# First value loads between weight pieces, rounding one piece ahead, a later input audit and a later flag product, in a fused recurrence and MLP kernel

## The chip, the cores and the metric

The kernel runs on one core of a Trainium2 chip. Its time is the device time of one execution in microseconds (us), given as the median of several runs. The profile of one execution gives the "span", from the first to the last instruction, which is about 2 us shorter than the device time. Engines: PE is TensorE, DVE is VectorE, ACT is ScalarE, POOL is GpSimd, SP issues the transfers.

## The reference

```python
# q, k, v, alpha: (4, 8, 768, 48), float32
for t in range(S):
    state = alpha[:, :, t, :, None] * state + einsum('bhd,bhe->bhde', k[:, :, t], v[:, :, t])
    y[:, :, t] = einsum('bhd,bhde->bhe', q[:, :, t], state)
x = y.transpose(0, 2, 1, 3).reshape(3072, 384)
h = x @ w_in                     # (384, 2048)
out = (h * sigmoid(h)) @ w_out   # (2048, 384)
```

The two weights arrive as 8-byte floats and are rounded to 4 bytes on the chip.

## The kernel before

Attention works on 24 chunks of 128 tokens, in "steps" of four slots. Between the slots the MLP is woven in as pieces: `enter` pieces (x times w_in, then Silu) and `leave` pieces (times w_out). Four places matter.

The start: the first inputs, four pieces of w_in and, further down, two pieces of v are loaded on one queue.

```python
    load(0)
    load(1)
    for _ in range(4):
        fetch()                  # w_in pieces, 512 KB each
    # ... constants ...
    for n in range(NV):
        load_v(n)                # 192 KB each, in rows of 48 floats
```

The rounding of one weight piece takes one ACT and three DVE instructions:

```python
            tc.keep_in_program_order(act.activation(up, lo, AF.Copy, scale=2.0**-29))
            w = dst.bitcast(I32)
            tc.keep_in_program_order(
                dve.tensor_scalar(w, hi, 3, 0x3FFFFFFF, ALU.logical_shift_left, ALU.bitwise_and))
            dve.scalar_tensor_tensor(w, hi, -(1 << 30), w, ALU.bitwise_and, ALU.bitwise_or)
            dve.tensor_tensor(w, w, up, ALU.add)
            fetch()
            yield
```

The audit reads alpha and the weights once more (37 items) to see that all values lie in the range in which the fast algorithm is exact. It has one buffer, so each turn is a load, then one or two DVE reductions. Two turns a step run from the 13th step on; the rest runs in the tail, with one or two MLP pieces between two turns:

```python
        if at % 2 == 0 and step > 3 * GB:          # GB = 4
            next(audits, None)
    # ...
    turns = 0
    while next(audits, 0) is None:
        turns += 1
        for _ in range(1 + turns % 2):
            go_on()                                # one MLP piece
```

The flag: the audit's outcome is summed over the partitions by a tiny matmul; each engine then reads it to choose whether a general version must run as well.

```python
    dve.tensor_reduce(good, ends, axis=AX, op=ALU.min)
    go_on()
    go_on()
    ps = ps_attn()[0:1, 0, 0:1]
    pe.matmul(ps, lhsT=good, rhs=mask[:, 0, C - 1 : C], start=True, stop=True)
    dve.tensor_single_scalar(small, ps, 127.5, ALU.is_ge)
    for _ in range(4):
        go_on()
    within = nc.values_load(small[0:1, 0:1], min_val=0, max_val=1)
```

The compiler reorders each engine's instructions, so program order is only roughly kept, except where the program pins an instruction behind those before it.

## Time and profile before

| | before |
|---|---|
| device time, median of 3 | 569.04 us (568.75 to 571.14) |
| span of the profiled execution | 567.3 us |
| PE busy | 549.0 us (97%) |
| DVE busy | 445.0 us (78%) |
| ACT busy | 205.4 us (36%) |
| chain that ended last | PE 69%, DVE 17%, DMA 9% |

With PE busy for 97% of the span, only its gaps can be won, and time in which its clock is low. The prediction below shows the table of busy time by stretch, PE's waits and the clock around the flag. A line number such as L794 is a line of that kernel; the changed kernel's lines are shifted by about 7. A line of a view in order of time gives the start and the duration in us, the engine, the line, the operation, output<-input, how many instructions (x4), and in brackets how long the engine stood idle before it and for what. "Evacuation" is the copying of finished sums out of one of PE's output banks, after which PE can use the bank again; L889 is DVE's addition on the output of an `enter` piece.

### The profile page before, as it was taken

Reading aid. Unit: us, or ns where it says so; the run is one execution under the profiler, and the core shown is the slowest. Engines: PE = TensorE matmul, PEld = TensorE weight load, DVE = VectorE, ACT = ScalarE, POOL = GpSimd, SP = SyncE. Lnnn points to the kernel's source line nnn. Section 1 sums busy time; section 2 is a strip of 40 time slices with the busy share of each in tenths; the row PEclk is TensorE's granted clock in tenths of the full one; section 3 lists DMA queues with packets and bytes.
Section 4 is the critical chain, followed back from the end, with each engine's and each line's share of the span. In section 5 each row is a group of like instructions: output and inputs, shape, how many; then the busy total and the mean of one; then the engine's idle time right before and its main releaser. Section 6 shows DMA issues by size and latency. Waiting matters only on the chain.

```text
span 567.3 us, 12315 instructions
## 1 busy us (share of the span) xinstructions
PE 549.0 (97%) x5026; PEld 489.4 (86%) x5026; DVE 445.0 (78%) x815; ACT 205.4 (36%) x407; POOL 14.6 (3%) x36
## 2 busy tenths in 40 slices
PE   6899999999999999899999999999999999998996
PEld 4777887678999999799989999998999999997995
DVE  5797898488898599996998897999995866746531
ACT  3555543134323342443433443434443241421200
POOL 4111000100000000000000000000000000000000
PEclk9999999999999999999999999999999999998999
DMA  9989981533243324444425544425431223331000
GB/s 229 205 242 221 217 191 36 136 103 82 70 113 100 83 64 108 126 130 111 132 69 159 143 111 127 135 75 157 127 97 44 66 69 99 92 116 44 14 29 25
DMA packets 94415, 63.78 MB, mean 112 GB/s; under 512 B 55312, under 2 KB 86032, under 8 KB 94352
## 3 DMA queue, kind: packets, MB, share of 16 engines
q1 hardware_dynamic: 94352, 62.94, 43.1%
q8 instruction: 40, 0.66, 0.5%
q14 instruction: 23, 0.19, 0.1%
HBM read 58.20 MB, written 4.72 MB: 111 GB/s over the span
## 4 chain that ended last, share of the span: by engine, by line
PE 69%; DVE 17%; DMA 9%; SPq 2%; issue 1%; ACT 1%; DVEq 0%; ACTq 0%
PE ps_o L973 25%; PE ps_m L875 15%; PE ps_m L852 13%; DMA bits<-in_moe_w_out_dram 6%; PE ps_a L794 6%; PE ps_o L1000 4%; DVE seen L657 3%; PE ps_a L751 3%; DVE turn L668 1%; DMA vn<-in_v_dram 1%; PE ps_a L768 1%; DVE g L889 1%; DVE g L978 1%; DVE p L722 1%; PE ps_a L688 1%
## 5 line engine op out<-in xcount | busy, mean ns | idle before, releaser
L973 PE MATMUL ps_o<-w_out,g 128*128 128x192 f32 x704 | 122.4, 328 | 0.0
L973 PEld LDWEIGHTS ps_o<-w_out,g 128*128 128x128 f32 x704 | 115.3, 190 | 2.3 <-issue 0.4
L973 PE MATMUL ps_o<-wt,g 128*128 128x192 f32 x528 | 92.0, 328 | 0.0
L852 PE MATMUL ps_m<-xt,w_in 128*128 128x256 f32 x384 | 89.2, 383 | 1.3 <-DVE w_in L621 0.7
L973 PEld LDWEIGHTS ps_o<-wt,g 128*128 128x128 f32 x528 | 88.2, 192 | 1.4
L852 PEld LDWEIGHTS ps_m<-xt,w_in 128*128 128x128 f32 x384 | 70.9, 190 | 11.9 <-DVE w_in L621 1.6
L875 PE MATMUL ps_m<-xc,w_in 128*128 128x256 f32 x288 | 70.1, 379 | 1.4 <-DVE g L889 1.4
L875 PEld LDWEIGHTS ps_m<-xc,w_in 128*128 128x128 f32 x288 | 54.0, 190 | 7.9 <-DVE g L889 1.7
L886 ACT ACTIVATE g<-g 128x1024 f32<-128x1024 f32 x32 | 33.0, 1054 | 59.1 <-DVE g L889 59.1
L657 DVE TENSOR_REDUCE seen<-bits 128x1 f32<-128x384 int32 (+2 forms) x65 | 42.4, 687 | 15.1 <-DMA bits<-in_moe_w_out_dram 14.9
L875 PE MATMUL ps_m<-xc,wx 128*128 128x256 f32 x192 | 50.4, 384 | 0.0
L881 ACT COPY g<-ps_m 128x512 f32<-128x512 f32 x64 | 36.8, 586 | 36.2 <-PE ps_m L875 36.2
L978 DVE TENSOR_TENSOR g<-g 128x512 f32<-128x512 f32 x66 | 44.4, 683 | 7.0 <-PE ps_o L973 7.0
L774 ACT ACTIVATE st<-st,least 128x96 f32<-128x96 f32 x80 | 24.0, 365 | 59.1 <-DVE least L696 59.1
L889 DVE TENSOR_TENSOR g<-ps_m,g 128x512 f32<-128x512 f32 x56 | 37.1, 680 | 2.3 <-PE ps_m L875 2.1
L875 PEld LDWEIGHTS ps_m<-xc,wx 128*128 128x128 f32 x192 | 34.9, 190 | 4.2 <-issue 0.4
L693 DVE TENSOR_TENSOR_SCAN u<-al,one 128x516 f32<-128x516 f32 x24 | 29.0, 1209 | 9.0 <-ACT al L690 8.9
L855 ACT ACTIVATE g<-ps_m 128x512 f32<-128x512 f32 x32 | 19.1, 596 | 41.8 <-PE ps_m L852 41.6
L722 DVE TENSOR_TENSOR_SCAN p<-al,inv 128x516 f32<-128x516 f32 x24 | 29.4, 1227 | 5.0 <-PE ps_a L794 4.7
L762 DVE TENSOR_TENSOR g<-ps_a,mask 128x512 f32<-128x512 f32 x40 | 25.7, 684 | 9.0 <-PE ps_a L751 8.7
L794 PE MATMUL ps_a<-g,vn 128*32 128x128 f32 x768 | 27.2, 282 | 2.4 <-DMA vn<-in_v_dram 2.4
L794 PEld LDWEIGHTS ps_a<-g,vn 128*32 128x32 f32 x768 | 20.3, 112 | 10.1 <-issue 8.4
(127 smaller groups left out, 654.7 us busy)
## 6 DMA issues: line engine op xcount, KB each, us to landing
bits<-in_moe_w_in_dram SPq DMA_DIRECT2D x24, 512.0 KB, 4.7
bits<-in_moe_w_out_dram SPq DMA_DIRECT2D x32, 384.0 KB, 3.3
at<-in_alpha_dram SPq DMA_DIRECT2D x64, 96.0 KB, 2.3
kt<-in_k_dram SPq DMA_DIRECT2D x64, 96.0 KB, 2.4
qt<-in_q_dram SPq DMA_DIRECT2D x64, 96.0 KB, 2.5
bits<-in_alpha_dram SPq DMA_DIRECT2D x9, 512.0 KB, 3.6
out_dram<-o SPq DMA_DIRECT2D x48, 96.0 KB, 1.7
an<-in_alpha_dram SPq DMA_DIRECT2D x8, 192.0 KB, 5.1
```

The source lines that it names most:

```text
L657: dve.tensor_reduce(seen[kind][which][:, i : i + 1], x, axis=AX, op=op, apply_absolute_value=True))
L693: dve.tensor_tensor_scan(u[:, end - 1 :: -1], sg[:, end:0:-1], one[:, end:0:-1], 0.0, ALU.mult, ALU.add)
L722: dve.tensor_tensor_scan(p[:, 0:end], sg[:, 0:end], iv[:, 0:end], 0.0, ALU.mult, ALU.add)
L762: dve.tensor_tensor(g[:, u].rearrange("p (o j) c -> p o j c", o=2), ps[u].rearrange("p (o j) c -> p o j c", o=2), m.to_broadcast([128, 2, ...
L794: pe.matmul(py[32 * at : 32 * at + 32, t, :], lhsT=w, rhs=x, start=(i < 4), stop=(i >= len(todo) - 4), skip_group_check=True)
L852: pe.matmul(ps[:, e, :], lhsT=w_in[:, t, (f + e) * 128 : (f + e + 1) * 128], rhs=xt[:, t, :], start=(t == 0), stop=(t == NKT - 1))
L875: pe.matmul(ps[:, e], lhsT=block_w(w)[:, 2 * pair + e], rhs=block_x(grp, x), start=(first and e == 0), stop=(e == 1), skip_group_check=True)
L881: act.copy(to, ps)
L886: act.activation(x, x, AF.Silu)
L889: dve.tensor_tensor(to, a, b, op)
L973: pe.matmul(ps, lhsT=x, rhs=w[:, i], start=(first and i == 0), stop=(i == HF - 1), skip_group_check=True)
L978: dve.tensor_tensor(cells(grp, h, pair, *to), cells(grp, h, pair, *x), cells(grp, h, pair, *y), ALU.subtract)
```

## The change

The intent: the first v no longer stands behind four large transfers; DVE no longer waits for ACT's rounding of the same piece; the audit leaves the stretch in which DVE is the bound; and the flag's product comes when its input is long there.

```diff
     load(0)
     load(1)
-    for _ in range(4):
+    for i in range(4):
         fetch()
+        if i % 2 == 0:
+            load_v(i // 2)
...
-    for n in range(NV):
-        load_v(n)
...
-        for dst, src in pieces:
+        def rounding(bits):
+            n = bits.shape[1]
+            up = upp.tile([128, 512], I32, name="up")[:, 0:n]
+            tc.keep_in_program_order(
+                act.activation(up, bits.bitcast(U32)[:, :, 0], AF.Copy, scale=2.0**-29))
+            return up
+        ahead = []
+        for i, (dst, src) in enumerate(pieces):
...
             bits = coming.pop(0)
+            up = ahead.pop() if ahead else rounding(bits)
...   (the three DVE instructions, as before)
+            if i + 1 < len(pieces):
+                ahead.append(rounding(coming[0]))
             fetch()
             yield
...
-        if at % 2 == 0 and step > 3 * GB:
+        if at % 2 == 0 and step > 3 * GB + 2:
             next(audits, None)
...
-    go_on()
-    go_on()
+    for _ in range(5):
+        go_on()
     ps = ps_attn()[0:1, 0, 0:1]
     pe.matmul(ps, lhsT=good, rhs=mask[:, 0, C - 1 : C], start=True, stop=True)
```

## The prediction

> **What bounds the kernel now.** I read the page's busy shares first, then busy time by stretch, then what TensorE waited for, then the order of time around each wait. TensorE (PE) is busy 549.0 of 567.3 us (97%). The table by stretch shows where it is not; columns are stretch, length, then busy time (and instructions) of PE, its weight loads, VectorE (DVE), ScalarE (ACT), GpSimd, then granted clock, DMA share, GB/s.
>
> ```profile
> 0.00:60.00 60.00, 51.59 (x506) 41.74 (x507) 44.86 (x78) 29.03 (x57) 12.45 (x33) 1.00 1.04 223
> 60.00:190.00 130.00, 129.81 (x1323) 107.84 (x1322) 104.16 (x195) 45.05 (x103) 2.17 (x3) 1.00 0.44 113
> 190.00:240.00 50.00, 48.22 (x545) 43.71 (x544) 46.33 (x92) 19.37 (x38) 0.00 (x0) 1.00 0.36 96
> 240.00:300.00 60.00, 59.65 (x560) 54.66 (x559) 55.19 (x95) 25.88 (x54) 0.00 (x0) 1.00 0.42 115
> 300.00:460.00 160.00, 159.96 (x1544) 146.52 (x1544) 140.04 (x252) 63.22 (x121) 0.00 (x0) 1.00 0.40 108
> 460.00:514.00 54.00, 54.00 (x294) 50.77 (x293) 33.52 (x63) 17.58 (x29) 0.00 (x0) 1.00 0.31 97
> 514.00:526.00 12.00, 9.89 (x46) 8.70 (x45) 7.04 (x19) 2.06 (x3) 0.00 (x0) 0.86 0.14 44
> 526.00:567.30 41.30, 35.89 (x221) 35.50 (x219) 13.82 (x27) 3.24 (x8) 0.00 (x0) 0.99 0.07 21
> ```
>
> Idle PE: 8.4 us before 60, 1.8 in 190-240, 0.35 in 240-300, 2.1 in 514-526, 5.4 after the last matmul. Nothing else is there to win, except a lower clock. The waits by cause (us in total, times, longest):
>
> ```profile
> PE ps_a L688 <- DMA an<-in_alpha_dram: 4.2, 1, 4.2
> PE ps_a L794 <- DMA vn<-in_v_dram: 2.4, 1, 2.4
> PE ps_a L1194 <- DVE good L1190: 2.1, 1, 2.1
> PE ps_m L875 <- DVE g L889: 1.8, 2, 1.4
> PE ps_m L852 <- DVE w_in L621: 0.7, 1, 0.7
> ```
>
> The first is the start-up load and stays. The other four are just what the four parts of the change aim at. The flag's wait costs more than its 2.1 us, as the clock (third number from the end) shows:
>
> ```profile
> 514.00:517.00 3.00, 0.89 (x8) 0.45 (x6) 1.79 (x9) 0.32 (x1) 0.00 (x0) 1.00 0.26 97
> 517.00:519.00 2.00, 2.00 (x10) 1.72 (x9) 1.22 (x5) 0.00 (x0) 0.00 (x0) 0.83 0.19 54
> 519.00:521.00 2.00, 2.00 (x7) 1.73 (x6) 1.78 (x4) 0.00 (x0) 0.00 (x0) 0.50 0.04 7
> 521.00:523.00 2.00, 2.00 (x11) 2.00 (x11) 0.67 (x2) 1.06 (x1) 0.00 (x0) 0.81 0.02 4
> ```
>
> In the chain of waits, 10 matmuls of 256 columns take 3.28 us and 16 of 192 take 3.36 there, against 2.16 and 2.60 at the usual 0.216 and 0.163 us each: 1.9 us lost to the clock.
>
> **What the Trainium skill says.** "TensorE: Matmul & The Clock Gate", section "What's actually happening": the array runs at half clock after an idle window of about 3.4 us and at full clock after a busy one. The trace agrees on the half rate (0.50) but shows it after only 2.1 us of idling, while 1.4 us at 232 us left the clock at 1.00. The same page, section "Architectural detail: the array is 16× 32×32, not 1× 128×128", calls ACT and DVE strict FIFOs. The trace agrees: the rounding copy at 36.84 us idled 2.21 us for its DMA, and the evacuation behind it began at 37.41 us though its matmuls had ended at 35.64. "DMA: Bandwidth & Descriptors", section "Queues, rings and completion order": each engine takes a queue's descriptors in ring order. The trace agrees: the four w_in pieces issued at 5.93, 7.12, 7.60 and 8.07 us land at 11.2, 12.4, 13.8 and 15.2, and the v behind them at 16.4. The same page, "Specifications", gives 512 bytes as the least transfer for line rate; v goes in rows of 192 bytes (48 floats), at about 165 GB/s in the trace against about 400 for w_in.
>
> **Part 1: v earlier.** The first v's load moves from behind four pieces to behind one: landing near 11.2 + 1.2 = 12.4 us instead of 16.4 (1.2 us is v's own time, 16.4 - 15.2). But PE also needs the masked scores:
>
> ```profile
> 13.11 1.07 ACT L757 COPY g<-ps_a 128x512 f32<-128x512 f32 x2 [1.22 <-PE ps_a L751]
> 13.76 1.40 POOL L758 TENSOR_SCALAR_AFFINE_SELECT g<-g 128x512 f32<-128x512 f32 x2 [6.75 <-ACT g L757]
> 16.53 1.94 PE L794 MATMUL ps_a<-g,vn 128*32 128x128 f32 x32 [2.41 <-DMA vn<-in_v_dram]
> ```
>
> GpSimd ends at 15.16 us, so at most 16.5 - 15.2 = 1.3 of the 2.4 us is free. The second to fourth w_in pieces land 1.2 to 2.4 us later than before.
>
> **Part 2: rounding one piece ahead.** The second rounding copy now stands on ACT before the scores' copies. It needs the second piece, which lands at 12.4 + 1.2 = 13.6 us, and takes 0.67: the copies then begin near 14.3 instead of 13.1, GpSimd ends near 16.4, and part 1 is eaten up (0.1 us left) unless the compiler lets the copies go first, which I can't see. In return DVE loses two waits for the roundings (2.01 us at 19.61 and 1.56 at 22.93). Most of that isn't on the path: DVE's next work, the scan at 23.54, needs an ACT copy that ends at 23.38, behind the same number of ACT instructions as before. From 27.6 to 33.6 us DVE converts three pieces without idling, and PE's 0.75 us at 33.65 hangs on the third. So both parts together shift the start by 0.2 to 1.5 us; I take 0.7.
>
> **Part 3: audit from the 15th step.** By the program's counts, two audit turns a step start at step 13 now; two steps less leave four turns for the tail. Between 204 and 252 us four reductions of 1.22 us (218.34, 229.07, 241.82, 250.96) leave DVE, which is 99% busy in 204-236. Two of them, 2.4 us, lie before the 1.77 us that PE waits at 233.7 and 235.3: that wait goes whole. The later 0.35 us at 297.88 goes too, since DVE is then 4.9 - 1.8 = 3.1 us further ahead. Gain 2.1 us. No work is removed; the reductions reappear in the tail, where DVE is 62% busy.
>
> **Part 4: the flag's product later.** In the tail the audit is a chain of one buffer: load 3.2 us, reduce 1.0. From 463.86 to 515.20 us are 12 turns, 4.28 us each. Four more turns end 17.1 us later, plus about 1 as one of them is a bigger w_in piece: the flag's input, at 516.8 now, comes at 534.9. PE's side: the loop of 17 instead of 13 turns runs 26 instead of 20 pieces, and 5 follow instead of 2, so nine more pieces precede the product, and 8 remain after it. Without its wait PE would come to the product at 514.8 + 2.2 (rest of a piece) + 2.6 + 1.7 + 6 x 2.6, or 536.9, both before the earlier gains, which shift both sides alike. So 2 us of slack, and no wait: gain 2.1 + 1.9 = 4.0 us. The branch still has 8 pieces, 21 us, to read the flag, whose loads take 0.5 us.
>
> Against it: DVE now waits for audit loads while the last output pieces run, whose products need DVE's subtractions two or three pieces (5 to 8 us) later, and whose first one needs a Silu that DVE feeds just in time (DVE ends at 526.1, the product runs from 525.3). A DVE held up to 3 us could stall PE there; I charge 0.8.
>
> Sum: 0.7 + 2.1 + 4.0 - 0.8 = 6.0 us; 569.0 - 6.0 = 563.0.
>
> **Rivals.** (a) *The flag waits again.* The chain may run slower than 4.28 us a turn beside output stores; at 4.8 the slack is gone, and a wait of 2 us may drop the clock again: gain only 2 to 3 us, 566.5. For it: only 2 us of slack; against: the w_in-sized turn is counted, and DMA is 7% busy there. (b) *DVE holds PE up in the last output pieces*, by 2 to 4 us in small stalls: 565 to 567. For it: DVE stood 1.2 to 2.7 us before each of the last reductions. Against: 460-514 has the same standing, with PE 54.00 of 54.00 us busy. (c) *The start gives more*: if the copies overtake the rounding, 1.3 us for v and DVE's 3.6 us freed let the conversions keep up, and the earlier full clock (32 matmuls take 1.94 us at 16.5, 1.08 later) adds some: 2.5 to 3.5 us in all, 560.5. (d) *ACT held by roundings for late pieces*, evacuations behind them: costs 1 us at most, ACT being 36% busy.
>
> **Range and chances.** Everything idle besides the start-up load and the end, with the clock loss, is 8.4 - 4.2 + 1.8 + 0.35 + 4.0 = about 10.4 us, below the 11.4 us that 2% needs; so faster by 2% is hardly possible. A loss of 2% would need a stall larger than any now in the trace. Worst likely: (a) with (b), 567; best: (c) with no stalls, 560.
>
> **What would show it.** Right: no wait of L1194 on L1190 and clock 1.00 throughout 510-560; no wait of L875 on L889 near 232; the wait of L794 replaced by one for GpSimd, with the first score copies after the second rounding; conversions without waits for the rounding; audit reductions until about 528. Wrong: a wait at the flag, PE gaps among the last L973, or the clock below 1.00 there.

## The result

The changed kernel took 564.79 us (median of 4, 564.23 to 565.42); the kernel before, run beside it, 569.69 us (568.75 to 571.14; the three executions of the table above and one more). The ratio is 0.9912 with a 95% interval of 0.9885 to 0.9939: within 2%, and faster.

The table by stretch of the changed kernel (same columns as in the prediction):

```profile
0.00:60.00 60.00, 50.67 (x509) 40.79 (x510) 45.52 (x79) 29.53 (x59) 12.64 (x33) 0.97 1.02 225
190.00:240.00 50.00, 49.89 (x556) 45.57 (x555) 46.83 (x94) 20.96 (x41) 0.00 (x0) 1.00 0.30 75
240.00:300.00 60.00, 59.66 (x592) 54.62 (x594) 53.14 (x92) 25.08 (x52) 0.00 (x0) 1.00 0.39 105
460.00:514.00 54.00, 53.58 (x289) 50.03 (x288) 33.77 (x65) 16.95 (x27) 0.00 (x0) 1.00 0.34 99
514.00:526.00 12.00, 11.40 (x65) 10.45 (x64) 10.40 (x21) 3.70 (x5) 0.00 (x0) 1.00 0.38 115
```

The gap of 1.8 us in 190-240 is nearly closed (49.89 of 50), and 514-526 holds 0.6 us of idling instead of 2.1. But 460-514, gapless before, now has a gap of 0.4 us, and the first 60 us have more idling than before (9.3 against 8.4 us). PE's waits by cause:

```profile
PE ps_a L695 <- DMA an<-in_alpha_dram: 4.1, 1, 4.1
PE ps_a L801 <- POOL g L765: 3.9, 2, 3.6
PE ps_o L980 <- DVE o L994: 0.9, 2, 0.5
PE ps_m L882 <- ACT g L888: 0.3, 1, 0.3
```

The waits for v, for the flag, for L889 and for the converted w_in (L621) are gone from the list. A wait for POOL's masking (3.9 us) has come instead of the one for v, and a new one, for the evacuation of an output bank by DVE (L994). The wait of 0.3 us for an ACT copy, which the prediction had going too, has stayed. The clock, where it was 0.83, 0.50 and 0.81 before:

```profile
517.00:519.00 2.00, 2.00 (x12) 1.70 (x10) 1.79 (x4) 0.15 (x1) 0.00 (x0) 1.00 0.00 1
519.00:521.00 2.00, 1.52 (x10) 1.26 (x8) 1.28 (x3) 1.59 (x2) 0.00 (x0) 1.00 0.70 240
521.00:523.00 2.00, 1.88 (x12) 1.59 (x12) 1.95 (x4) 0.68 (x2) 0.00 (x0) 1.00 0.02 6
```

It is at full rate here. The start, in order of time, with the second rounding (L610), the scores' copies (L764), POOL's masking and the first values matmuls:

```profile
13.71 0.66 ACT L610 ACTIVATE up<-bits 128x512 int32<-128x512 uint32 x1 [1.64 <-DMA bits<-in_moe_w_in_dram]
14.28 1.05 ACT L764 COPY g<-ps_a 128x512 f32<-128x512 f32 x2
14.91 1.95 POOL L765 TENSOR_SCALAR_AFFINE_SELECT g<-g 128x512 f32<-128x512 f32 x2 [7.90 <-ACT g L764]
15.89 0.64 PE L801 MATMUL ps_a<-g,vn 128*32 128x128 f32 x4 [3.62 <-POOL g L765]
16.92 1.71 PE L801 MATMUL ps_a<-g,vn 128*32 128x128 f32 x26 [0.24 <-POOL g L765]
```

The copies wait behind the second rounding, which waits for the second piece until 13.7 us, as foretold: most values matmuls still start at 16.9 us, though v itself was issued at 7.13 and needs 5.3 us to land.

To compare traces I use three marks: when PE begins the values matmuls of one attention step near 191 us, those of the step near 235 us (two steps on), and the end of the span. Before: 191.29, 236.32, 567.3. Changed: 190.66, 233.76, 562.7. So the trace has 0.6 us gained at the start, 1.9 in the middle and 2.0 in the rest. Whether 0.6 us of one trace can be trusted is one of the questions of the experiments.

### The profile page after: what moved, and what is told of

Read it like the earlier page. It is cut to its first block, busy times and chain, and to the rows that moved or that the text cites. A ratio compares the mean times of both kernels' runs of the same rounds, so it can differ in the third digit from the quotient of the medians.

```text
span 562.7 us, 12315 instructions
## 1 busy us (share of the span) xinstructions
PE 546.2 (97%) x5026; PEld 486.5 (86%) x5026; DVE 445.6 (79%) x815; ACT 205.3 (36%) x407; POOL 14.8 (3%) x36
## 4 chain that ended last, share of the span: by engine, by line
PE 70%; DVE 15%; DMA 9%; issue 2%; ACT 2%; SPq 2%; POOL 0%; DVEq 0%; ACTq 0%
PE ps_o L980 25%; PE ps_m L859 14%; PE ps_m L882 14%; DMA bits<-in_moe_w_out_dram 7%; PE ps_a L801 6%; PE ps_o L1007 4%; PE ps_a L758 3%; DVE seen L664 3%; PE ps_a L775 1%; DVE g L896 1%; DVE turn L675 1%; DVE g L985 1%; DMA bits<-in_moe_w_in_dram 1%; PE ps_a L695 1%; PE ps_a L816 1%
## 5 line engine op out<-in xcount | busy, mean ns | idle before, releaser
L896 DVE TENSOR_TENSOR g<-ps_m,g 128x512 f32<-128x512 f32 x56 | 37.4, 685 | 0.7 <-PE ps_m L882 0.5
L801 PE MATMUL ps_a<-g,vn 128*32 128x128 f32 x768 | 28.4, 282 | 3.9 <-POOL g L765 3.9
```

The costliest lines, as they stand in the source:

```text
L801: pe.matmul(py[32 * at : 32 * at + 32, t, :], lhsT=w, rhs=x, start=(i < 4), stop=(i >= len(todo) - 4), skip_group_check=True)
L896: dve.tensor_tensor(to, a, b, op)
```

## The experiments

My theory: the start parts are worth 0.6 us at most because the rounding ahead eats what the earlier v gives; the audit's shift gives 1.9 us in the middle; the flag's later product gives 4.0 us (2.1 of waiting and 1.9 of low clock); and 1.8 us of this go to stalls in the tail, as DVE stands before audit loads while output pieces need it. The rivals: the clock's dip has nothing to do with the flag; the parts simply add up; the audit's shift only moves time; rounding ahead helps. All eleven runs were timed with 5 rounds, in three calls on three chips, and all gave correct results. The first call held a_flag, b_audit, c_start and d_no_round, the second h_tail, e_no_v, f_second and after_again, the third g_14th, k_v_flag and d_again; they had before at 569.67, 570.92 and 569.46 us. Medians compare well only within a call; between calls the ratio to before is the fairer measure. "Middle" is the time between the first two marks, "rest" that from the second mark to the span's end.

| run | parts in it | median us | ratio to before | 191 mark | middle | rest |
|---|---|---|---|---|---|---|
| before | none | 569.04 | 1 | 191.29 | 45.03 | 330.98 |
| changed | all four | 564.79 | 0.9912 | 190.66 | 43.10 | 328.94 |
| a_flag | flag | 566.87 | 0.9950 | 192.03 | 45.03 | 328.04 |
| b_audit | audit | 568.24 | 0.9978 | 192.18 | 43.10 | 331.22 |
| c_start | v, rounding | 571.09 | 1.0018 | 191.36 | 45.98 | 331.86 |
| d_no_round | v, audit, flag | 563.69 | 0.9894 | 189.57 | 43.10 | 328.93 |
| h_tail | audit, flag | 565.65 | 0.9907 | 192.22 | 43.08 | 329.20 |
| e_no_v | rounding, audit, flag | 566.13 | 0.9916 | 192.42 | 43.09 | 329.49 |
| f_second | all, but rounding ahead only from the third piece | 563.84 | 0.9879 | 189.53 | 43.10 | 329.17 |
| after_again | all four | 565.70 | 0.9911 | 193.24 | 43.09 | 329.17 |
| g_14th | v, flag, audit from the 14th step | 563.13 | 0.9885 | 190.49 | 43.09 | 327.52 |
| k_v_flag | v, flag | 563.71 | 0.9895 | 189.70 | 45.05 | 327.15 |
| d_again | v, audit, flag | 563.87 | 0.9889 | 190.10 | 43.08 | 329.12 |

### a_flag: the flag's product later, nothing else

```diff
-    go_on()
-    go_on()
+    for _ in range(5):
+        go_on()
     ps = ps_attn()[0:1, 0, 0:1]
```

> The kernel before with the flag's product three pieces later and nothing else. Theory (the flag's 2.1 us wait also halves the clock for a while, 1.9 us more): a gain of 3.5 to 4.1 us over before, no wait at the flag's product, granted clock 1.00 from 510 to 550. Rival 1 (the clock's dip is not this wait's doing): a gain of 2.1 us and the dip still there. Rival 2 (most of the change's gain lies in the audit's shift): under 1.5 us.

Measured: 566.87 us against 569.67, 2.8 us faster (ratio 0.9950, interval 0.9928 to 0.9973). There is no wait at the product, and the granted clock is 1.00 in every stretch from 460 us on. Rival 1 falls, as the dip left together with the wait, and so does rival 2; but the gain is below the range that I gave. The rest of the trace is 2.9 us shorter, not 4.0: against k_v_flag, which has the same audit and flag, the first output piece after the last `enter` piece takes 3.25 us instead of 3.00, and the stretch from the second mark up to it is 0.6 us longer. That the compiler's order of instructions makes this difference is a guess.

### b_audit: the audit from the 15th step, nothing else

```diff
-        if at % 2 == 0 and step > 3 * GB:
+        if at % 2 == 0 and step > 3 * GB + 2:
```

> The kernel before with the audit from the 15th step and nothing else. Theory: TensorE passes the attention step near 236 us 1.9 us earlier, but four more audit turns of 4.28 us follow in the tail against six more pieces of 2.6 us, so the wait at the flag grows from 2.1 to 4 to 6 us, and the clock dip with it: slower than before by 0.5 to 4 us. Rival (the parts add up independently): faster by 1.9 us.

Measured: 568.24 us, 1.4 us faster than before (ratio 0.9978, interval 0.9955 to 1.0002, which leaves "no change" possible). The middle is 1.93 us shorter, as both sides had it. The expectation that the flag's wait would grow failed:

```profile
PE ps_a L1194 <- DVE good L1190: 1.6, 1, 1.6
PE ps_o L973 <- DVE o L987: 1.3, 2, 0.7
```

The wait is 1.6 us. The compiler put the product 12 matmuls later among PE's instructions than the program has it, so 2 us of the wait were filled, and PE arrived later anyway because of two new stalls of 0.7 and 0.6 us for DVE's evacuation of an output bank. The rest of the trace is 0.2 us longer than before. I had reckoned with the program's place of the product; in b_audit's trace it isn't there.

### c_start: the two start parts alone

```diff
-        if at % 2 == 0 and step > 3 * GB + 2:
+        if at % 2 == 0 and step > 3 * GB:
...
-    for _ in range(5):
-        go_on()
+    go_on()
+    go_on()
```

(from the changed kernel)

> The change's two start parts alone (v between the pieces, rounding one ahead), audit and flag as before. Theory: 0.6 us gained up to 190 us and kept to the end: 568.9 when before is 569.5. Rival (the 2.4 us wait for v was on the path whole): 2 us or more.

Measured: 571.09 us (569.24 to 573.09), ratio 1.0018 with 1 inside the interval: no gain. The rival falls, and the theory's 0.6 us doesn't show either. The profile adds something that I hadn't looked for. PE's wait of 1.4 and 0.4 us for L896 (L889 before) is the same as in the kernel before, but the clock behind it isn't:

```profile
231.00:234.00 3.00, 1.61 (x10) 1.32 (x9) 3.00 (x8) 0.00 (x0) 0.00 (x0) 1.00 0.71 206
234.00:237.00 3.00, 2.60 (x8) 1.66 (x7) 3.00 (x7) 1.06 (x1) 0.00 (x0) 0.73 0.56 135
237.00:240.00 3.00, 3.00 (x89) 2.51 (x88) 2.31 (x4) 2.61 (x4) 0.00 (x0) 0.70 0.22 66
```

Here the clock fell to 0.73 and 0.70, and the middle took 45.98 us instead of 45.03. In the traces of before, a_flag and k_v_flag the same wait left it at 1.00. So whether a gap of 1.4 us costs clock differs between these executions. At the flag, c_start repeats what the kernel before does: PE waits 2.25 us, and the four matmuls after it, 1.03 us otherwise, take 1.91:

```profile
519.98 1.91 PE L882 MATMUL ps_m<-xt,wx 128*128 128x256 f32 x4
```

So the low clock stands behind the flag's wait in both traces where this wait lasted over 2 us, it is absent in b_audit, where the wait lasted 1.6 us, and absent in all ten traces with the product late.

### d_no_round and d_again: the changed kernel without rounding ahead

```diff
-            if i + 1 < len(pieces):
-                ahead.append(rounding(coming[0]))
```

> The changed kernel without rounding ahead (v, audit and flag as changed). Theory: the scores' copies go right after the first rounding, GpSimd's masking ends near 14 us, the first values matmuls start by 14.5 instead of 15.9 to 16.9, and TensorE passes 190 us 0.5 to 1.5 us earlier than the changed kernel does: faster than it by that. Rival (the roundings ahead are what freed the start): slower than the changed kernel by 0.3 us or more, with VectorE waiting for roundings again.

> v early, flag late, audit from the 15th step, no rounding ahead: the same program as d_no_round, for comparison on this chip. 563.7 within 0.5; over 1 us faster than the changed kernel's 564.8 to 565.7, with 190 us passed near 189.6.

Measured: 563.69 us (ratio 0.9894) and, in the third call, 563.87 us (0.9889): faster than the changed kernel by 1.1 us against its first result and by 1.8 against its second. These are comparisons between calls; the ratios make it 1.0 and 1.3 us, and f_second below settles it within one call. The copies go right after the first rounding and POOL is done at 15.2:

```profile
13.14 1.07 ACT L762 COPY g<-ps_a 128x512 f32<-128x512 f32 x2 [1.05 <-PE ps_a L756]
13.79 1.40 POOL L763 TENSOR_SCALAR_AFFINE_SELECT g<-g 128x512 f32<-128x512 f32 x2 [6.78 <-ACT g L762]
14.48 0.64 PE L799 MATMUL ps_a<-g,vn 128*32 128x128 f32 x4 [0.32 <-POOL g L763]
```

The values matmuls start at 14.5 and 15.3 us instead of 15.9 and 16.9. POOL ends at 15.2, a little later than the 14 that I expected. DVE does wait for roundings again (0.68 and 0.92 us), but since that waiting isn't on the path, the 191 mark comes at 189.6 and 190.1 (d_again was expected near 189.6). The rival falls: the rounding ahead isn't what freed the start, it is what blocked it.

### h_tail: audit and flag alone

```diff
     (the kernel before with the edits of a_flag and b_audit)
```

> The change's audit and flag parts alone, start as before. Theory (1.9 us for the audit, 4.0 for the flag, 1.8 lost to small stalls in the tail): 4.1 us faster than before. If it comes out equal to the changed kernel (564.8), the two start parts together are worth nothing; theory from the traces says they are worth 0.6 us at most.

Measured: 565.65 us, 5.3 us below before, more than the 4.1 that I expected. The changed kernel, in the same call, took 565.70, so the two start parts together are worth nothing that can be measured (the means differ by 0.3 us, the ranges overlap).

A comparison that I had not planned: h_tail is a_flag plus the audit's shift. Its middle is 1.95 us shorter than a_flag's, its rest only 1.16 longer, so in this pair of traces the shift gains 0.8 us. The two were timed in different calls (ratios 0.9907 and 0.9950).

### e_no_v: rounding ahead without the earlier v

```diff
-    for i in range(4):
-        fetch()
-        if i % 2 == 0:
-            load_v(i // 2)
+    for _ in range(4):
+        fetch()
...
+    for n in range(NV):
+        load_v(n)
```

> The changed kernel with v loaded late as before (roundings one ahead, audit and flag as changed). Theory: the second piece lands at 12.4 us, so the rounding ahead is over before the scores' copies at 13.1 and delays nothing, but the values matmuls wait for v until 16.4: TensorE passes 190 us within 0.4 us of where the kernel before does, 565.0 to 565.6. Rival (rounding ahead gains by itself, VectorE being freed of 3.6 us of waiting): 564 or less.

Measured: 566.13 us (565.81 to 566.84), 0.5 us slower than h_tail and a little above the range that I gave. The 191 mark lies at 192.42 against 192.22. PE waits 2.4 us for v, as before. Rounding ahead doesn't help by itself; the rival falls.

### f_second: the second piece rounded in its own turn

```diff
-            if i + 1 < len(pieces):
+            if (which or i) and i + 1 < len(pieces):
                 ahead.append(rounding(coming[0]))
```

> The changed kernel, but the second piece is rounded in its own turn and only from the third on one ahead. Theory: the scores' copies go before the second rounding, so the start is as quick as without rounding ahead (first values matmuls at 14.5 us, 190 us passed about 1.1 us sooner than in the changed kernel): 563.7, and 0 to 0.5 us better still if the later roundings ahead help. Rival (any rounding ahead blocks ScalarE, not just the second one): close to 564.8.

Measured: 563.84 us, 1.9 us below the changed kernel of the same call, with the 191 mark at 189.53, within 0.04 us of d_no_round's. So it is the second piece's rounding alone that costs the time, and no effect of the roundings ahead of the later pieces shows. The rival, that any rounding ahead blocks ScalarE, falls.

### after_again: how far the same code varies

> The changed kernel itself once more, beside the others on one chip: 564.8, within 0.4; tells how far the first values matmuls and the passing of 190 us vary between executions of the same code (I expect up to 0.7 us, by when the clock rises).

Measured: 565.70 us, 0.9 us above its first result, so outside the 0.4 that I allowed; the ratio to before is the same (0.9911 against 0.9912), as before was slower too. The spread of the start is larger than I had expected: this trace has the 191 mark at 193.24, 2.6 us later than the first trace of the same program. (The traced execution, 567.24 us, shares the slowest time of the six.) The four transposes of the third chunk's alpha show why, in the changed kernel's first trace and in this one:

```profile
21.14 0.66 PE L695 MATMUL ps_a<-ident,an 128*128 128x128 f32 x4
```

```profile
22.50 1.06 PE L695 MATMUL ps_a<-ident,an 128*128 128x128 f32 x4
```

The array runs them in 0.66 us at full rate, in 1.06 at about half. In the first trace it had reached full rate by 8.9 us and dipped once more after the 3.6 us gap; in this one it was slow until 26 us. Starts as in the kernel before vary too, by 0.9 us: 191.29, 192.03, 192.18 and 192.22 in four traces with the same start code. The 0.6 us that two single traces gave for the start was therefore within this variation, and h_tail is what settles it.

### k_v_flag: the audit back at the 13th step

```diff
-        if at % 2 == 0 and step > 3 * GB + 2:
+        if at % 2 == 0 and step > 3 * GB:
```

(from d_no_round)

> v early and flag late, no rounding ahead, audit from the 13th step as before. Theory: the 1.8 us wait at 232 us is back and the tail's stalls are fewer: 1.2 to 1.9 us slower than with the audit from the 15th step. Rival (the audit's shift only moves time from the middle to the tail): equal within 0.4 us.

Measured: 563.71 us, against 563.87 for d_again. The rival holds and the theory's size falls: with the flag's product late and this start, moving the audit is worth nothing. (With the old start, a_flag and h_tail above, the traces show 0.8 us. The changed kernel with the audit at the 13th step was not run.) The wait near 232 us is back,

```profile
232.15 1.13 PE L880 MATMUL ps_m<-xc,w_in 128*128 128x256 f32 x4 [1.39 <-DVE g L894]
233.68 1.13 PE L880 MATMUL ps_m<-xt,w_in 128*128 128x256 f32 x4 [0.41 <-DVE g L894]
```

and the middle takes 45.05 us instead of 43.08; but the rest takes 327.15 instead of 329.12. The 2.0 us that leave the middle come back in the tail to the last tenth. In the changed kernel's trace one such stall looks as follows, in order of time, first on DVE and then on PE:

```profile
517.21 1.01 DVE L664 TENSOR_REDUCE seen<-bits 128x1 f32<-128x384 int32 x2 [0.76 <-DMA bits<-in_moe_w_out_dram]
518.13 0.68 DVE L896 TENSOR_TENSOR g<-ps_m,g 128x512 f32<-128x512 f32 x1
518.73 0.68 DVE L567 SCALAR_TENSOR_TENSOR g<-g 128x512 f32<-128x512 f32 x1
519.33 0.35 DVE L994 TENSOR_TENSOR o<-ps_o,u 128x192 f32<-128x192 f32 x1
519.74 3.25 PE L980 MATMUL ps_o<-w_out,g 128*128 128x192 f32 x16 [0.48 <-DVE o L994]
```

DVE stands 0.76 us before an audit load and reduces for 1.0 us; what the MLP needs has queued up behind, and the evacuation that frees PE's next bank comes at 519.33, 0.5 us too late. The piece itself takes 3.25 us instead of k_v_flag's 3.00, since its Silu is late as well. At the other stall, near 482 us, DVE waited for no load: the reduction's own duration is enough to make the evacuation (L994) late:

```profile
482.19 1.02 DVE L664 TENSOR_REDUCE seen<-bits 128x1 f32<-128x384 int32 x2
483.12 0.35 DVE L994 TENSOR_TENSOR o<-ps_o,u 128x192 f32<-128x192 f32 x1
```

k_v_flag's trace has no wait for this evacuation at all. In d_again's trace the two waits (0.49 and 0.53 us) and the longer piece (0.25) are 1.3 of the 2.0 us.

### g_14th: the audit from the 14th step

```diff
-        if at % 2 == 0 and step > 3 * GB + 2:
+        if at % 2 == 0 and step > 3 * GB + 1:
```

(from d_no_round)

> v early and flag late, no rounding ahead, audit one step sooner (from the 14th). Theory: both reductions that lay before the wait near 233 us are still gone (the first would fall after it), and two audit turns less stand in the tail, so the stalls there (0.4 at 482, 0.5 and 0.5 at 519 to 522 us) shrink by up to half: 0 to 0.7 us faster than with the 15th step. Rival (the step's worth is the sheer number of reductions in the thirteenth to fifteenth steps): up to 1 us slower, with the wait for L889 back.

Measured: 563.13 us (562.64 to 564.25), 0.7 us below d_again and 0.6 below k_v_flag: the lowest median, though f_second, in another call, has the lower ratio to before (0.9879 against 0.9885). The wait near 232 us doesn't return (middle 43.09), no evacuation stall is left in the tail, and the rest takes 327.52 us. After the 191 mark this trace is 1.6 us shorter than d_again's and k_v_flag's (370.6 us, from 561.1 less 190.49, against 372.2 for both); its start, which is the same code, was 0.4 to 0.8 us slower. The timed gap of 0.7 us is less than that and the ranges overlap, so its size remains uncertain. The rival falls.

## Why the prediction was right or wrong

The prediction was right: 564.79 us lies between the 560 and the 567 that it gave as best and worst, and the change stayed below the 2% that it called hardly possible. The forecast of 563.0 was 1.8 us too low, and the steps differ in how well they held. Its signs of being right came out, but for a wait of 0.2 us for a rounding; so did one sign of being wrong: a gap among the last output pieces (0.48 us at 519.74).

**v earlier, and rounding ahead: mechanism right, balance wrong.** The landing near 12.4 us (7.13 + 5.3), the second piece near 13.6 (it landed at 13.7), the copies near 14.3 (14.28) and POOL's end near 16.4 (16.86) all came as worked out. The landings agree with the ring order that the Trainium skill gives ("DMA: Bandwidth & Descriptors", section "Queues, rings and completion order"): with v issued behind one piece instead of four it was no longer waited for, and the second piece landed at 13.7 us instead of 12.4. "So both parts together shift the start by 0.2 to 1.5 us; I take 0.7" is the term that was mis-sized: h_tail and after_again measure 0.0 within some tenths. The part that I couldn't see, which of the two instructions the compiler would let go first on ACT, fell on the unfavourable side. The two single effects are larger: dropping the rounding ahead of the second piece gives 1.9 us (f_second against after_again), and v earlier without that rounding gives 1.8 us (f_second against h_tail, same call), more than the 1.3 us that I had put as the most the earlier v could free. In those starts PE began most values matmuls 1.6 us sooner (15.3 against 16.9 us) and reached full rate between 18 and 20 us, against about 20 to 26 in the others. That the clock accounts for the difference is the likely reading, and wasn't tested by itself.

**Audit: right in the middle, wrong as a sum.** "That wait goes whole", 1.77 us, measured 1.93 to 1.95 in every trace with the audit shifted. The further 0.35 us that the prediction added stayed: the trace of the kernel before already gave it as a wait for an ACT copy (L881), so it was misread as one that DVE's lead would end. The step says that "the reductions reappear in the tail", where DVE has room, and the share of busy time made that look harmless. A share of busy time doesn't say when DVE is needed: a reduction, with or without a wait for its load before it, makes an evacuation late that PE is about to need.

**Flag: right.** No wait at the product and no dip, in all traces with it late. Against the 4.0 us of the prediction, k_v_flag's rest is 3.8 us shorter than before's, a_flag's 2.9. The audit chain's pace of 4.28 us a turn held exactly: from 461.27 to 529.77 us the changed kernel makes 16 turns. Its flag's input was ready at 532.0 us and the product ran at 535.9, so the slack was 3.9 us, not 2.

**Stalls in the tail: right in kind, too small.** "I charge 0.8" is the second mis-sized term. d_again's rest is 2.0 us longer than k_v_flag's, which differs only in the audit's start; h_tail's is 1.2 longer than a_flag's. The named place was right (the first output piece, its Silu and its bank), but rival (b), held against by the argument that 460-514 had been gapless before, was the better forecast there: 0.4 us near 482 us is in just that stretch.

With the measured terms, 0.0 + 1.9 + 3.8 - 2.0 = 3.7 us. With the old start's traces it is 1.95 + 2.94 - 1.16, or 3.7 us as well, so the sum is firmer than its split between the flag and the tail. The traces after the 191 mark give 3.7 to 4.0 (376.0 before against 372.0 and 372.3). The timed difference is larger, 4.9 us in the first comparison. About 1 us of it thus comes from outside the prediction's terms, and that the forecast missed by only 1.8 us is luck to this extent. The runs with a wait at the flag spread more than the others: before 566.8 to 573.5 us in the third call and 569.24 to 573.09 for c_start, against 0.8 to 2.0 us for every kernel without it. A clock that falls behind a wait in some executions and not in others would do that, and c_start's profile shows such a case; but only one execution of each kernel is traced. The record does give every execution's mean granted clock: in the third call the four fastest of before (566.8 to 568.74 us) read 0.997 to 1.000, the four slowest (570.87 to 573.5) 0.986 to 0.992. That fits; but in the first call the relation is weak, and c_start's six all read 0.992 or 0.993 over a spread of 3.9 us. So the spread's cause remains argued, not shown. That b_audit spread only 2.2 us, with no dip in its trace, fits.

Open: why a_flag gains 0.9 us less in the rest than k_v_flag with the same audit and flag; no run separates that. With it stays open whether the audit's shift is worth nothing or 0.8 us in the changed kernel itself.

## What to carry to other kernels

When a change moves work off the engine that bounds one stage, ask which instruction of that engine another one will wait for where the work lands: here 2 us left the middle and 1.2 to 2 us came back in the tail, because a reduction of 1.0 us, in part after a wait for its load, stood on DVE before an evacuation that PE needed. The same holds for rounding ahead on ACT: an instruction pulled ahead should have its input by then, or be kept behind the work on the critical path. And a short wait of TensorE can cost as much again in clock (here 2.1 us of waiting and 1.9 of low clock; of five waits of 1.4 to 1.6 us four cost none), so removing one may pay twice; effects below 1 us should then be judged by paired timing, not by two single traces.

## What the Trainium skill lacked or had wrong

- "TensorE: Matmul & The Clock Gate", section "What's actually happening", has the clock fall after about 3.4 us of idling. Here 2.1 us of idling at the flag were followed by 0.50 in the kernel before, 2.25 us by 0.50 in c_start, and gaps of 1.4 and 0.4 us by 0.73 and 0.70 in c_start, while the same gaps left it at 1.00 in before, a_flag and k_v_flag. The page does say that the window runs freely, which fits the variation; in these traces gaps shorter than the window were nonetheless followed by a low clock.
- The same page calls the cost of the ramp small and variable. Its size here: up to 2.6 us between two executions of the same program at the 191 mark (190.66 and 193.24), 0.5% of the time. What the page lacks is that this spoils comparisons of start code by single traces.
- Same page: in the first 20 us the profile's granted clock reads 1.00 (before, after_again) while the matmuls run at about half rate (1.08 to 1.12 us for four transposes, 0.66 once warm). The page, section "Seeing it yourself", warns that the clock's trace events are unreliable; that the half rate of a start can go unrecorded isn't said.
